# Exponential steps of three and two score tiles in turn, on fixed sets of PSUM banks

## The chip, the cores and the metric

The kernel runs on one core of one Trainium2 chip. Five engines work side by side: TensorE (PE, matmuls; its weight loads are PEld), ScalarE (ACT), VectorE (DVE), GpSimd (POOL) and SyncE (SP, which here only issues DMAs). They share SBUF, and PSUM with eight banks of 512 float32 values on each of 128 partitions. The metric is device time in microseconds of the whole program, the median of several runs.

## What is computed

```python
xn = layernorm(A_x)                                  # 2048 rows x 640
q = (xn @ wq) in 32 heads of 20;  k = xn @ wk;  v = xn @ wv    # one key and value head for all
p = softmax(q k^T * 20**-0.5);  A = concat_heads(p v) @ wo
h = relu(xn @ w1 + b1) ** 2;    B = h @ w2 + b2      # 640 -> 1536 -> 640
out = A_x + A + B
```

The attention is the larger part: 32 heads x 2048 queries x 2048 keys, 134 million exponentials.

## The kernel before

**Tiles.** The work of attention is cut into blocks of four heads and 512 queries: 8 x 4 = 32 blocks. A block has 16 key tiles (kt) of 128 keys. So a block has 64 score tiles (128 keys x 512 queries, exactly one PSUM bank), and the kernel 2048. A score matmul has only 20 rows of contraction, so the array is used in its row mode there, and up to four heads' matmuls run side by side. All other matmuls run in column mode, as four matmuls of 32 columns side by side.

**Two ways to an exponential.** A score tile goes one of two ways:

- ScalarE takes two or three neighbouring banks in one step (`make_act`, line 861) and writes exp as bf16 to the ring `PT` of 20 slots. TensorE then multiplies with the values (`make_pv`), four matmuls for a key tile.
- VectorE approximates: four score tiles of a key tile form a *set*. Each is turned into the bit pattern of a bf16 number by one multiply-add (`D1`, line 1036). Three further patterns are made from all four at once by adding a constant (*passes*, `P1` to `P3`, line 1054, on GpSimd or VectorE). TensorE multiplies all four patterns with scaled values (`make_dpv`), sixteen matmuls for a key tile.

**The value product** of a block collects in one PSUM bank, `PVB` = 7. When all 16 key tiles are in, VectorE copies it out (`TN`, line 929), and small DMAs and VectorE operations divide by the sum of the exponentials. The first value product of the next block waits for that copy.

**Other work** is cut into units: transposes, projections of keys, values and queries, the two layers of the feed-forward part, and the output. A unit takes one PSUM bank, some column matmuls and one eviction by VectorE.

**Order.** Nothing of the order is written out by hand. A planner in the kernel's Python picks one operation after the other with modelled durations and puts it at the end of its engine's queue; the program then has that order for good. The parts that the change touches:

- `make_step` chooses the banks of a step of ScalarE. `STATIC` is off, so it takes any two neighbouring banks of 0 to 6 that come free soonest, or three if at least five are free.
- `pool_banks` gives the banks for VectorE's score tiles (`make_dqk`) and for units: any of 0 to 6.
- When a score step is issued, `make_dqk` may add score tiles for VectorE to it in the same slot of TensorE, until four heads are busy.
- `new_set` opens a set only if enough of the block is left for it to finish. `back` is what GpSimd still has to do; of its queue only passes count.
- `tail_bank` chooses banks for the last half rows of the output.
- Where TensorE would stand idle, the planner adds *fillers*, matmuls of zeros into the open value bank (`fill_parts`), or warm-up matmuls before the first one (`warm_parts`).

All matmuls of these parts are issued through one helper, line 318, so their rows in the profile are told apart by their tiles: `ps<-qT,kT` are scores, `ps<-PT,vx` ScalarE's value products, `ps<-tmore,...` and `ps<-x_sb,...` those of the sets (x_sb's space is reused for patterns), `ps<-kT,zeros` fillers.

Of the kernel before, what the change touches and what calls it, by code (L numbers as in the profile page):

```python
# [16 lines left out]
NBLK = QC * G  # L17
# [18 lines left out]
def _pl(z):  # L36
# [6 lines left out]
XB = (127.0 - EXP_SHIFT * LOG2E - math.log2(TNORM)) * 128.0  # L43

PTR = 20
NB = 7
PVB = 7
SHARED = (4, 5, 6)
STATIC = False
SIDES = ((0, 1), (2, 3))  # L50
POOLED = tuple(range(NB))
HELD = sum(SIDES, ())
EVP = 0.8
JIT = 0.8
# [24 lines left out]
ACTEV = (0, 2)  # L79
KEEP = 1  # L80
DJIT = 9.0
RULES = {}
HOOK = None
PRIO = {'XN1': 0.13}
# [23 lines left out]
MODEL = {}  # L108

DEFAULTS = dict(EVP=EVP, PBIAS=PBIAS, MPRIO=MPRIO, DGAP=DGAP, DLAST=DLAST, DRATE=DRATE, BEHIND=BEHIND, IDLE=IDLE, URG=URG, NOPEN=NOPEN,  # L110
                EPS=0.03, JIT=JIT, R3=R3, STATIC=STATIC, PVA=1, PVD=1, D1P=1, PP=4, SQP=2, DQP=3, QKP=0, ND=2, WARM=WARM, KEEP=KEEP, DJIT=DJIT)


class Ctr:
# [61 lines left out]
def bass_parallel_sum__grouped_kv_mqa__dense_activation_squared_relu__prompt_kernel(nc, A_x, A_wq, A_wk, A_wv, A_wo, B_x, B_w1, B_b1, B_w2, B_b2, out):  # L176
    es = ExitStack()
    with es:
# [276 lines left out]
        DUM = Op("first", "PE", 0.0, [])  # L455

        def fill_parts():
            return [mm(ps[32 * jj:32 * jj + 32, PVB, :], zeros32[:, :], kT[:, 0:512], False, False, (0, 32 * jj)) for jj in range(4)]

        def warm_parts():  # L460
            return [lambda e: e.matmul(ps[:, PVB, :], ones_bf[:, :], hT_tmp[:, 0, :], start=True, stop=True)]

        def need_te(sts):
            return [te_op[st] for st in sts]
# [335 lines left out]
        def make_step():  # L800

            j = len(steps)
            if par("STATIC"):
                banks = list(SIDES[j % 2])
                if any(bank_state(bk) is None for bk in banks):
                    return None
                return build_step(j, banks, 0.0)
            t0 = max(free["PE"], horizon() - par("JIT"))
            st_of = {bk: bank_state(bk) for bk in range(NB)}
            ok = [bk for bk in range(NB) if st_of[bk] is not None and st_of[bk] <= t0 + 0.02]  # L810
            banks = None
            if len(ok) >= 3 + par("R3"):
                ap = [(a, a + d, a + 2 * d) for d in (1,) for a in range(NB - 2 * d) if {a, a + d, a + 2 * d} <= set(ok)]
                if ap:
                    banks = list(ap[0])
            if banks is None:
                can = sorted((max(st_of[bk], st_of[bk + 1], t0), bk) for bk in range(NB - 1) if st_of[bk] is not None and st_of[bk + 1] is not None)
                if not can:
                    return None
                banks = [can[0][1], can[0][1] + 1]  # L820
            return build_step(j, banks, t0)
# [41 lines left out]
        def after_act(st_):  # L863
            for k, t in enumerate(st_["tiles"]):
# [5 lines left out]
                if kt_left[key] == 0:  # L870
                    pv_ready[key[0]].append(("A", key[1]))

        def make_pv(b, kt):
            first, last = b not in pv_begun, pv_count[b] == KT - 1
            parts, deps = [], []
            for h in range(HPG):
                o, sl = tile_act[(b, kt, h)]
                deps.append(o)
                parts.append(mm(ps[32 * h:32 * h + 32, PVB, :], vx[:, kt, :], PT[:, sl, :], first, last, (0, 32 * h)))
            deps.append(v_op[kt // 4])  # L880
            if first and b > 0:
                deps.append(tn_op[b - 1])
            return Op(f"PV{b}_{kt}", "PE", 0.222, parts, deps)

        def make_dpv(s, term):
            b, kt, n = s["b"], s["kt"], s["n"]
            first, last = b not in pv_begun, pv_count[b] == KT - 1 and len(s["terms"]) == 1
            src, wgt = tbuf(s["buf"][term]), (vx if term == 0 else vxs[:, term - 1, :, :])
            deps = list(s["made"][term])
            parts = []  # L890
            for h in range(HPG):
                i = s["order"].index(h)
                parts.append(mm(ps[32 * h:32 * h + 32, PVB, :], wgt[:, kt, :], src[:, i * 512:(i + 1) * 512], first, last, (0, 32 * h)))
            deps.append(v_op[kt // 4])
            if term:
                deps.append(vs_op[kt // 4][term - 1])
            if first and b > 0:
                deps.append(tn_op[b - 1])
            return Op(f"DPV{b}_{kt}_{term}", "PE", 0.2205, parts, deps)

        def finish_pv(b, o):
# [12 lines left out]
        def emit_norm(b, lastpv):  # L914
            marg = DMARG if b < NBLK - 3 else DMEND
            qc, g = divmod(b, G)
            a = b % NOR
            if b >= NBLK - 2:
                Tn, T2 = OR[:, a, :], QCr[:, 0, :]
                tn = op(f"TN{b}", "DVE", 0.63, lambda e: e.transpose(out=Tn, in_=ps[:, PVB, :]), [lastpv] + or_users[a], prio=0)  # L920
                rc = op(f"RC{b}", "DVE", 0.155, lambda e: e.reciprocal(out=Tn[:, DH:512:32], in_=Tn[:, DH:512:32]), [tn], prio=0)
                tm = op(f"TM{b}", "DVE", 0.6, lambda e: e.tensor_tensor(out=T2.rearrange("p (c d) -> p c d", d=32), in0=Tn.rearrange("p (c d) -> p c d", d=32),
                                                                        in1=Tn.rearrange("p (c d) -> p c d", d=32)[:, :, DH:DH + 1].to_broadcast([128, 16, 32]),
                                                                        op=ALU.mult), [rc] + [d for k in qc_dma for d in qc_dma[k]], lock=True, prio=0)
                tn_op[b] = tn
                a = b - NBLK + 2
                tb_op[(qc, NCH - 1 + a)] = op(f"TB{b}", "DVE", 0.63, lambda e: e.transpose(out=OTE[:, a, :], in_=T2), [tm], prio=0)
                return
            tn = op(f"TN{b}", "DVE", 0.60, lambda e: e.tensor_copy(out=OR[:, a, :], in_=ps[:, PVB, :]), [lastpv] + or_users[a], prio=0)
            tn_op[b] = tn  # L930
            d1 = op(f"SM{b}", "SP", 0.58, lambda e: e.dma_start(drs[b, 0].rearrange("(j n) -> j n", j=HPG), OR[DH:128:32, a, :]), [tn], lat=3.1 + marg, dma=nsum[a])
            d2 = op(f"SL{b}", "SP", 0.5, lambda e: e.dma_start(R4[:, a, :], drs[b, 0].rearrange("(p n) -> p n", p=128)), [d1, r4_user.get(a)], lat=1.6 + marg, dma=nr4[a])
# [33 lines left out]
        def new_set():  # L966
            b = cur["b"]
            now = free["PE"]
            opn = sum(1 for s in sets[-NL:] if s["left"])
            back = max(free["POOL"] - now, 0.0) + sum(o.dur for o in pool_q if o.blk is not None) + opn * 1.5 * 1.86  # L970
            need = max(back, HPG * par("DRATE") * (1 + opn)) + par("DLAST")
            if len(unclaimed[b]) * HPG * 0.4523 * 0.85 + DSLACK <= need:
                b += 1
            if b >= NBLK or not (b == 0 or b in qt_op):
                return None
            ok = [kt for kt in unclaimed[b] if kt_ok(kt) and kt // 4 in vs_op]
            if not ok:
# [12 lines left out]
            return s  # L990

        def pool_banks():

            if par("STATIC"):
                return [bk for bk in POOLED if bk not in HELD and bank_state(bk) is not None]
            fb = [bk for bk in POOLED if bank_state(bk) is not None]
            return fb if len(fb) > par("KEEP") else []

        def pick_bank(fb):
# [70 lines left out]
        def tail_bank():  # L1070
            done = not peek_tiles(1)[0]
            bs = [bk for bk in range(NB) if (bk not in HELD or done) and bank_state(bk) is not None]
            if tn_op.get(NBLK - 1) is not None and tn_op[NBLK - 1].fin is not None and not bank_busy[PVB]:
                bank_rel[PVB] = bank_rel[PVB] or tn_op[NBLK - 1]
                bs.append(PVB)
            return min(bs, key=lambda bk: (bank_state(bk), bk)) if bs else None

        def tail_ops():
# [66 lines left out]
        while True:  # L1145
# [34 lines left out]
                if rd is not None and (nq is None or nq > max(free["PE"], rd) + par("DGAP")):  # L1180
                    consider("PE", par("DQP"), r[0], ("dqk",) + r[1:])
            b = pv_blk[0]
            if b < NBLK and (b == 0 or b - 1 in tn_op):
                for k, (kind, x) in enumerate(pv_ready[b]):
                    if kind == "A":
                        consider("PE", par("PVA"), make_pv(b, x), ("pv", b, k))
# [73 lines left out]
            elif kind == "qk":  # L1260
                take_step(ap[1])
                heads = [t[2] for t in ap[1]["tiles"]]
                while len(heads) < HPG:
                    r = make_dqk(heads)
                    if r is None:
# [9 lines left out]
            elif kind == "dqk":  # L1275
                after_dqk(o, *ap[1:])
            elif kind == "pv":
                pv_begun.add(ap[1])
                pv_of[(ap[1], pv_ready[ap[1]].pop(ap[2])[1])] = o
                finish_pv(ap[1], o)  # L1280
            elif kind == "dpv":
                pv_begun.add(ap[1])
                s_, term = ap[3], ap[4]
                s_["pv"][term] = o
                s_["terms"].remove(term)
# [126 lines left out]
```

## Time and profile before

| | before |
|---|---|
| median of 3 runs | 719.19 us (718.53 to 721.15) |
| profiled execution, time and span | 718.53 us, span 716.7 us |
| exponential steps on ScalarE, two tiles and three tiles | 722 and 16 |
| score tiles evicted by VectorE | 556 |
| passes on GpSimd, on VectorE | 216, 201 |
| filler matmuls of zeros | 52 |
| first exponential, start | 14.55 us |
| granted TensorE clock | 1.0 |

How to read the rows: "L861 ACT ACTIVATE PT<-ps 128x1024 x722 | 666.9, 1185 | 7.5" is line, engine, operation, output and input, count, then the time in which the engine was busy with the group, the mean time of one in ns, and the idle time before. Consecutive operations of an engine overlap in part, so the mean of one times the count can exceed the busy time. An "x4" after a matmul counts single matmuls, and four make a group.

### The profile page before, as it was taken

How to read it: one execution, taken by the hardware profiler on the slowest of the kernel's cores; microseconds unless marked ns; L12 is line 12 of the kernel's file. 1: busy time of each engine (PE TensorE's matmuls, PEld its weight loads, DVE VectorE, ACT ScalarE, POOL GpSimd, SP SyncE). 2: the span in 40 equal slices, each digit the busy share in tenths (PEclk: the TensorE clock that was granted, in tenths of full speed). 3: DMA queues.
4: the chain of work that ended last, by engine and by line, in shares of the span. 5: the costliest groups of instructions: out<-in, count | busy, mean ns of one | idle time of the engine just before them, and what ended most of it. 6: DMA issues, size and time to landing. Idle time of an engine off the chain costs nothing.

```text
span 716.7 us, 22623 instructions
## 1 busy us (share of the span) xinstructions
PE 705.8 (98%) x9787; PEld 219.6 (31%) x9789; DVE 642.5 (90%) x1100; ACT 694.1 (97%) x760; POOL 439.3 (61%) x274
## 2 busy tenths in 40 slices
PE   8999999999999999999999999999999999999998
PEld 4422222233322223333322223333333222233234
DVE  7879999998999989897999989999999999999973
ACT  6899999999999999999999999999999899999994
POOL 3727667758577664564457457667757557575643
PEclk9999999999999999999999999999999999999999
DMA  6416411332357501112110001101111100221101
GB/s 197 116 51 172 117 35 58 99 92 57 97 107 159 140 17 26 41 54 57 39 27 19 24 22 28 49 22 47 29 49 47 29 21 22 90 56 28 53 17 48
DMA packets 42016, 44.01 MB, mean 61 GB/s; under 512 B 15540, under 2 KB 32772, under 8 KB 41788
## 3 DMA queue, kind: packets, MB, share of 16 engines
q1 hardware_dynamic: 39132, 36.93, 18.9%
q0 software_dynamic: 2208, 5.25, 3.5%
q8 instruction: 77, 1.26, 0.7%
q10 hardware_dynamic: 576, 0.38, 0.2%
q14 instruction: 23, 0.19, 0.1%
HBM read 28.03 MB, written 14.91 MB: 60 GB/s over the span
## 4 chain that ended last, share of the span: by engine, by line
ACT 71%; PE 25%; DVE 2%; DMA 1%; issue 0%; SPq 0%
ACT PT L861 71%; PE ps L318 24%; DVE tmore L1036 1%; DMA x_sb<-in_A_x_dram 1%; PE ps L491 1%; DVE tmore L1054 0%; PE ps L519 0%; DVE x_sb L1054 0%; PE ps L447 0%; ACT OC L372 0%; SPq L335 0%; DVE OC L955 0%; PE ps L426 0%; SPq L342 0%; ACT xnT L428 0%
## 5 line engine op out<-in xcount | busy, mean ns | idle before, releaser
L861 ACT ACTIVATE PT<-ps 128x1024 bf16<-128x1024 f32 (+1 forms) x738 | 684.3, 1194 | 8.5 <-PE ps L318 8.3
L1036 DVE TENSOR_SCALAR tmore<-ps 128x512 uint16<-128x512 f32 x556 | 358.8, 682 | 36.6 <-PE ps L318 33.1
L1054 POOL TENSOR_SCALAR tmore<-tmore 128x2048 uint16<-128x2048 uint16 x115 | 217.1, 1896 | 154.3 <-PE ps L318 57.3
L318 PE MATMUL ps<-qT,kT 20*128 20x512 bf16 x2048 | 291.3, 384 | 4.4 <-ACT PT L861 3.0
L1054 POOL TENSOR_SCALAR x_sb<-tmore 128x2048 uint16<-128x2048 uint16 x101 | 190.6, 1896 | 88.7 <-DVE x_sb L1054 34.2
L318 PEld LDWEIGHTS ps<-qT,kT 20*128 20x128 bf16 x2048 | 74.3, 91 | 289.7 <-ACT PT L861 239.3
L318 PE MATMUL ps<-PT,vx 128*32 128x512 bf16 x1492 | 138.2, 386 | 0.0
L1054 DVE TENSOR_SCALAR x_sb<-tmore 128x2048 uint16<-128x2048 uint16 x129 | 98.8, 794 | 0.5 <-PE ps L318 0.5
L318 PE MATMUL ps<-x_sb,vxs 128*32 128x512 bf16 x920 | 82.5, 382 | 0.0
L318 PE MATMUL ps<-w_sb,big 128*32 128x320 bf16 x1536 | 77.3, 302 | 0.3 <-DVE tmore L1036 0.3
L318 PE MATMUL ps<-xnT,w_sb 128*32 128x512 bf16 x960 | 75.9, 384 | 0.5 <-ACT PT L861 0.4
L318 PE MATMUL ps<-tmore,vxs 128*32 128x512 bf16 x748 | 67.4, 382 | 0.0
L318 PEld LDWEIGHTS ps<-PT,vx 128*32 128x32 bf16 x1492 | 35.9, 94 | 61.5 <-issue 54.4
L318 PE MATMUL ps<-tmore,vx 128*32 128x512 bf16 x556 | 54.4, 383 | 0.0
L1054 DVE TENSOR_SCALAR tmore<-tmore 128x2048 uint16<-128x2048 uint16 x72 | 53.1, 750 | 0.2 <-PE ps L318 0.2
L318 PEld LDWEIGHTS ps<-w_sb,big 128*32 128x32 bf16 x1536 | 31.6, 95 | 32.0 <-issue 24.7
L599 DVE TENSOR_SCALAR hT_tmp<-ps,b1col 128x512 bf16<-128x512 f32 x48 | 35.7, 745 | 3.7 <-PE ps L318 3.4
L318 PE MATMUL ps<-xnT,wq_sb 128*32 128x512 bf16 (+1 forms) x480 | 34.1, 356 | 0.0
L318 PE MATMUL ps<-wo_c,OC 128*32 128x320 bf16 x608 | 31.1, 301 | 0.0
L607 DVE TENSOR_TENSOR big<-hT_tmp 128x512 bf16<-128x512 bf16 x48 | 27.0, 573 | 0.2
L318 PEld LDWEIGHTS ps<-x_sb,vxs 128*32 128x32 bf16 x920 | 21.4, 95 | 18.8 <-issue 12.9
L318 PEld LDWEIGHTS ps<-xnT,w_sb 128*32 128x32 bf16 x960 | 17.8, 94 | 28.0 <-issue 22.5
(82 smaller groups left out, 263.3 us busy)
## 6 DMA issues: line engine op xcount, KB each, us to landing
xbd<-b2d SPq DMA_DIRECT2D x16, 320.0 KB, 4.3
xbd<-in_A_x_dram POOLq DMA_DIRECT2D x8, 640.0 KB, 6.7
xr<-xbd SPq DMA_DIRECT2D x32, 160.0 KB, 2.4
w_sb<-in_B_w_dram SPq DMA_DIRECT2D x8, 480.0 KB, 4.7
big<-OR SPq DMA_DIRECT2D x71, 40.0 KB
big<-drs SPq DMA_DIRECT2D x71, 40.0 KB
out_dram<-out_sb SPq DMA_DIRECT2D x15, 160.0 KB, 1.9
qT<-QCr SPq DMA_DIRECT2D x108, 20.0 KB
```

Source lines behind the costliest of these rows:

```text
L318: return lambda e: e.matmul(out_, l, r, start=start, stop=stop, tile_position=tp)
L491: return [(lambda e, dt=dt: e.transpose(out=psbf(bk)[:, dt * 128:(dt + 1) * 128], in_=xn_sb[:, st, dt:D:DT], identity=ident[:])) for dt in ...
L599: o = Op(f"RL{qc}_{f}", "DVE", 0.66, [lambda e: e.tensor_scalar(out=hT_tmp[:, k % 2, :], in0=ps[:, bk, :], scalar1=b1col[:, f:f + 1], scal ...
L607: q = op(f"SQ{qc}_{f}", "DVE", 0.34, lambda e: e.tensor_tensor(out=h2T[:, f, :], in0=hT_tmp[:, k % 2, :], in1=hT_tmp[:, k % 2, :], op=ALU. ...
L861: return Op(f"ACT{st_['j']}", "ACT", 0.05 + 0.4267 * n, [lambda e: e.activation(out=PT[:, s0:s0 + n, :], in_=ps[:, b0:b0 + (n - 1) * db + ...
L1036: d1 = op(f"D1_{n}_{i}", "DVE", 0.60, lambda e: e.tensor_scalar(out=L[:, cs].bitcast(U16), in0=ps[:, bank, :], scalar1=XA, scalar2=XB, op0 ...
L1054: p = op(f"P{j}_{n}", eng, 0.60 if eng == "DVE" else 1.86, lambda e, T=T, j=j, two=two: e.tensor_scalar(out=T.bitcast(U16), in0=L.bitcast( ...
```

## The change

The eight banks are split for good. Banks 0, 1, 2 and banks 3, 4 are two sets (`SIDES`) that ScalarE's steps take in turn, three tiles and two tiles; banks 5, 6, 7 are for VectorE's score tiles, for units and for the value product. The value product has no fixed bank any more: at the first product of a block `bank_for` chooses one of the three, `kept` keeps it from other use before that, and the first product waits for that bank's last reader. `back` counts everything that GpSimd has queued. The tail may use any of the eight banks. `DV` belongs to a branch that joins two steps of two and that runs only with `STATIC` off.

```diff
-NB = 7
-PVB = 7
+NB = 8
+PV0 = 7
 SHARED = (4, 5, 6)
-STATIC = False
-SIDES = ((0, 1), (2, 3))
+STATIC = True
+SIDES = ((0, 1, 2), (3, 4))
 POOLED = tuple(range(NB))
 HELD = sum(SIDES, ())
...
+DV = 9
+D1P = 1
...
+        pv_bank = {0: PV0}
+        bank_busy[PV0] = True
+
+        def bank_for(b):
+
+            if b in pv_bank:
+                return pv_bank[b]
+            can = [(bank_state(bk), -bk) for bk in range(NB) if bank_state(bk) is not None and not (par("STATIC") and bk in HELD)]
+            return -min(can)[1] if can else None
+
+        def kept():
+
+            b = pv_blk[0]
+            return bank_for(b) if b < NBLK and b not in pv_begun else None
+
+        def pv_begin(b):
+            if b not in pv_begun:
+                pv_bank[b] = bank_for(b)
+                bank_busy[pv_bank[b]] = True
+                pv_begun.add(b)
...
-            if first and b > 0:
-                deps.append(tn_op[b - 1])
+            if first:
+                deps.append(bank_rel[bank])
...
+            tn.frees = pb
...
-            back = max(free["POOL"] - now, 0.0) + sum(o.dur for o in pool_q if o.blk is not None) + opn * 1.5 * 1.86
+            back = max(free["POOL"] - now, 0.0) + sum(o.dur for o in pool_q) + opn * 1.5 * 1.86
...
+            keep = kept()
             if par("STATIC"):
-                return [bk for bk in POOLED if bk not in HELD and bank_state(bk) is not None]
-            fb = [bk for bk in POOLED if bank_state(bk) is not None]
+                return [bk for bk in POOLED if bk not in HELD and bk != keep and bank_state(bk) is not None]
+            fb = [bk for bk in POOLED if bk != keep and bank_state(bk) is not None]
...
             bs = [bk for bk in range(NB) if (bk not in HELD or done) and bank_state(bk) is not None]
-            if tn_op.get(NBLK - 1) is not None and tn_op[NBLK - 1].fin is not None and not bank_busy[PVB]:
-                bank_rel[PVB] = bank_rel[PVB] or tn_op[NBLK - 1]
-                bs.append(PVB)
...
-            if b < NBLK and (b == 0 or b - 1 in tn_op):
+            if b < NBLK and (b == 0 or b - 1 in tn_op) and bank_for(b) is not None:
```

With `STATIC` on, `make_step` takes the banks from `SIDES`, and a step is possible only when the whole set of its turn is free in the planner's books:

```python
            if par("STATIC"):
                banks = list(SIDES[j % 2])
                if any(bank_state(bk) is None for bk in banks):
                    return None
                return build_step(j, banks, 0.0)
```

More of the change, by code (lines that the diff above doesn't have):

```diff
@@ L110 @@
 DEFAULTS = dict(EVP=EVP, PBIAS=PBIAS, MPRIO=MPRIO, DGAP=DGAP, DLAST=DLAST, DRATE=DRATE, BEHIND=BEHIND, IDLE=IDLE, URG=URG, NOPEN=NOPEN,
-                EPS=0.03, JIT=JIT, R3=R3, STATIC=STATIC, PVA=1, PVD=1, D1P=1, PP=4, SQP=2, DQP=3, QKP=0, ND=2, WARM=WARM, KEEP=KEEP, DJIT=DJIT)
+                EPS=0.03, JIT=JIT, R3=R3, STATIC=STATIC, PVA=1, PVD=1, D1P=D1P, PP=4, SQP=2, DQP=3, QKP=0, ND=2, WARM=WARM, KEEP=KEEP, DJIT=DJIT, DV=DV)
 class Ctr:
@@ L457, in fill_parts @@
         def fill_parts():
-            return [mm(ps[32 * jj:32 * jj + 32, PVB, :], zeros32[:, :], kT[:, 0:512], False, False, (0, 32 * jj)) for jj in range(4)]
+            return [mm(ps[32 * jj:32 * jj + 32, pv_bank[pv_blk[0]], :], zeros32[:, :], kT[:, 0:512], False, False, (0, 32 * jj)) for jj in range(4)]
         def warm_parts():
-            return [lambda e: e.matmul(ps[:, PVB, :], ones_bf[:, :], hT_tmp[:, 0, :], start=True, stop=True)]
+            return [lambda e: e.matmul(ps[:, PV0, :], ones_bf[:, :], hT_tmp[:, 0, :], start=True, stop=True)]
         def need_te(sts):
@@ L808, in make_step @@
             t0 = max(free["PE"], horizon() - par("JIT"))
-            st_of = {bk: bank_state(bk) for bk in range(NB)}
+            keep = kept()
+            st_of = {bk: bank_state(bk) if bk != keep else None for bk in range(NB)}
             ok = [bk for bk in range(NB) if st_of[bk] is not None and st_of[bk] <= t0 + 0.02]
@@ L875, in make_pv @@
             parts, deps = [], []
+            bank = bank_for(b)
             for h in range(HPG):
@@ L878, in make_pv @@
                 deps.append(o)
-                parts.append(mm(ps[32 * h:32 * h + 32, PVB, :], vx[:, kt, :], PT[:, sl, :], first, last, (0, 32 * h)))
+                parts.append(mm(ps[32 * h:32 * h + 32, bank, :], vx[:, kt, :], PT[:, sl, :], first, last, (0, 32 * h)))
             deps.append(v_op[kt // 4])
-            if first and b > 0:
-                deps.append(tn_op[b - 1])
+            if first:
+                deps.append(bank_rel[bank])
             return Op(f"PV{b}_{kt}", "PE", 0.222, parts, deps)
@@ L890, in make_dpv @@
             parts = []
+            bank = bank_for(b)
             for h in range(HPG):
                 i = s["order"].index(h)
-                parts.append(mm(ps[32 * h:32 * h + 32, PVB, :], wgt[:, kt, :], src[:, i * 512:(i + 1) * 512], first, last, (0, 32 * h)))
+                parts.append(mm(ps[32 * h:32 * h + 32, bank, :], wgt[:, kt, :], src[:, i * 512:(i + 1) * 512], first, last, (0, 32 * h)))
             deps.append(v_op[kt // 4])
@@ L896, in make_dpv @@
                 deps.append(vs_op[kt // 4][term - 1])
-            if first and b > 0:
-                deps.append(tn_op[b - 1])
+            if first:
+                deps.append(bank_rel[bank])
             return Op(f"DPV{b}_{kt}_{term}", "PE", 0.2205, parts, deps)
@@ L917, in emit_norm @@
             a = b % NOR
+            pb = pv_bank[b]
             if b >= NBLK - 2:
                 Tn, T2 = OR[:, a, :], QCr[:, 0, :]
-                tn = op(f"TN{b}", "DVE", 0.63, lambda e: e.transpose(out=Tn, in_=ps[:, PVB, :]), [lastpv] + or_users[a], prio=0)
+                tn = op(f"TN{b}", "DVE", 0.63, lambda e: e.transpose(out=Tn, in_=ps[:, pb, :]), [lastpv] + or_users[a], prio=0)
+                tn.frees = pb
                 rc = op(f"RC{b}", "DVE", 0.155, lambda e: e.reciprocal(out=Tn[:, DH:512:32], in_=Tn[:, DH:512:32]), [tn], prio=0)
@@ L928, in emit_norm @@
                 return
-            tn = op(f"TN{b}", "DVE", 0.60, lambda e: e.tensor_copy(out=OR[:, a, :], in_=ps[:, PVB, :]), [lastpv] + or_users[a], prio=0)
+            tn = op(f"TN{b}", "DVE", 0.60, lambda e: e.tensor_copy(out=OR[:, a, :], in_=ps[:, pb, :]), [lastpv] + or_users[a], prio=0)
+            tn.frees = pb
             tn_op[b] = tn
@@ L992, in pool_banks @@
         def pool_banks():
+            keep = kept()
             if par("STATIC"):
-                return [bk for bk in POOLED if bk not in HELD and bank_state(bk) is not None]
-            fb = [bk for bk in POOLED if bank_state(bk) is not None]
+                return [bk for bk in POOLED if bk not in HELD and bk != keep and bank_state(bk) is not None]
+            fb = [bk for bk in POOLED if bk != keep and bank_state(bk) is not None]
             return fb if len(fb) > par("KEEP") else []
@@ L1262, in bass_parallel_sum__grouped_kv_mqa__dense_activation_squared_relu__prompt_kernel @@
                 heads = [t[2] for t in ap[1]["tiles"]]
+                if len(heads) == 2 and not par("STATIC") and sum(1 for bk in POOLED if bank_state(bk) is not None and bank_state(bk) <= o.start + 0.06) >= par("DV"):
+                    can = [bk for bk in range(NB - 1) if all(k != kept() and bank_state(k) is not None and bank_state(k) <= o.start + 0.06 for k in (bk, bk + 1))]
+                    st_ = build_step(len(steps), [can[0], can[0] + 1], 0.0) if can else None
+                    if st_ is not None and len(st_["tiles"]) == 2 and not set(t[2] for t in st_["tiles"]) & set(heads):
+                        rd = st_["qk"].ready()
+                        if rd is not None and rd <= o.start + 0.06:
+                            st_["qk"].dur = 0.005
+                            commit(st_["qk"])
+                            st_["qk"].lat = 0.425
+                            take_step(st_)
+                            heads += [t[2] for t in st_["tiles"]]
                 while len(heads) < HPG:
@@ L1277, in bass_parallel_sum__grouped_kv_mqa__dense_activation_squared_relu__prompt_kernel @@
             elif kind == "pv":
-                pv_begun.add(ap[1])
+                pv_begin(ap[1])
                 pv_of[(ap[1], pv_ready[ap[1]].pop(ap[2])[1])] = o
@@ L1281, in bass_parallel_sum__grouped_kv_mqa__dense_activation_squared_relu__prompt_kernel @@
             elif kind == "dpv":
-                pv_begun.add(ap[1])
+                pv_begin(ap[1])
                 s_, term = ap[3], ap[4]
```

## The prediction

> **What bounds the kernel now.** I read the page's busy times first.
>
> ```profile
> PE 705.8 (98%) x9787; PEld 219.6 (31%) x9789; DVE 642.5 (90%) x1100; ACT 694.1 (97%) x760; POOL 439.3 (61%) x274
> ```
>
> ScalarE (ACT) and TensorE (PE) are both full, so I need to know which of them a step of the loop waits for. The groups with shapes kept apart give ScalarE's two kinds of step (two and three tiles of 512 scores) and VectorE's eviction of a score tile:
>
> ```profile
> L861 ACT ACTIVATE PT<-ps 128x1024 bf16<-128x1024 f32 x722 | 666.9, 1185 | 7.5 <-PE ps L318 7.3
> L861 ACT ACTIVATE PT<-ps 128x1536 bf16<-128x1536 f32 x16 | 25.5, 1593 | 1.0 <-PE ps L318 1.0
> L1036 DVE TENSOR_SCALAR tmore<-ps 128x512 uint16<-128x512 f32 x556 | 358.8, 682 | 36.6 <-PE ps L318 33.1
> ```
>
> 722 x 2 + 16 x 3 = 1492 tiles go through ScalarE and 556 through VectorE, together 2048. The mean of a step is longer than its share of the busy time, because the write of one step overlaps the read of the next. What counts is the distance from start to start, and the chain that ended last gives it:
>
> ```profile
> 39.97 243.76 ACT PT L861 x263
> ...
> 354.95 165.05 ACT PT L861 x179
> ...
> 520.04 31.68 PE ps L318 x451
> ...
> 709.07 4.15 PE ps L318 x116
> ```
>
> By the trace's records six of the 263 steps and two of the 179 have three tiles. So 257a + 6b = 243.76 and 177a + 2b = 165.05, which gives a = 0.918 us for a step of two and b = 1.33 us for a step of three. The single records agree: a step of three is followed after 1.330 us in most of the sixteen cases, a step of two at best after 0.904 us. A tile more costs 0.426 us, an instruction more only 0.904 - 2 x 0.426 = 0.052 us. The stretch from 520 us shows that TensorE ends the chain in places. The waits say who is late:
>
> ```profile
> PEld ps L318 <- ACT PT L861: 242.8, 610, 0.8
> ...
> PEld ps L318 <- DVE tmore L1036: 15.1, 45, 0.6
> ...
> ACT PT L861 <- PE ps L318: 8.3, 7, 2.1
> ```
>
> Score matmuls wait for ScalarE 610 times, mostly to be allowed into a bank that ScalarE is still reading. ScalarE stood idle for TensorE only 7 times. Last, the timeline of TensorE around one score step:
>
> ```profile
> 159.03 0.39 PE L318 MATMUL ps<-tmore,vxs 128*32 128x512 bf16 x4
> ...
> 159.35 0.39 PE L318 MATMUL ps<-qT,kT 20*128 20x512 bf16 x2
> ...
> 159.67 0.40 PE L318 MATMUL ps<-PT,vx 128*32 128x512 bf16 x4
> ...
> 159.89 0.39 PE L318 MATMUL ps<-tmore,vx 128*32 128x512 bf16 x4
> ```
>
> A group of four column matmuls takes 0.22 us (159.67 to 159.89). From the group before the score step to the one after are 0.64 us, so a score step costs 0.42 us, with its two changes of the array's mode. Before, 942 groups of 512 columns for the value products and fillers and 340 for projections, 1282 x 0.2225 = 285 us, and 552 groups of 320 columns x 0.138 = 76 us, make 0.490 us a step; with 0.42 that is 0.91 us, which is ScalarE's own pace. The two are balanced.
>
> **The change part by part.** The order of the built program settles the counts. ScalarE has 320 steps of three and 320 of two, 1600 tiles: 108 more than before, in 98 fewer instructions. VectorE has 448 evictions at line 1036 for 556 (112 sets for 139), and GpSimd 137 passes for 216, VectorE's own passes 199 for 201.
>
> *More tiles on ScalarE.* Why: three of eight banks are left to all else, one of them holds the running value product, and the rule that opens a set now counts all that GpSimd has queued. Cost on the path: 108 x 0.426 = 46.0 us, less 98 x 0.052 = 5.1 us, is 40.9 us. ScalarE is busy without a break for most of the span, so nothing hides it.
> The page "ScalarE: Activation LUTs" of the Trainium skill, section Rules for kernel authors, budgets about 0.3 us per ACTIVATE plus 0.83 ns per element. By its fixed part 98 fewer instructions would give back 29 us and leave the kernel only some 16 us slower, an estimate from that page. Back to back, this trace shows 0.052 us, since most of the fixed part lies under the next step, and I go by the trace.
>
> *Less on VectorE and GpSimd.* 108 evictions x 0.682 = 74 us and 79 passes x 1.896 (mean of GpSimd's passes) = 150 us go away. Both engines already wait for others, so this is worth nothing directly; what is late next is still ScalarE.
>
> *TensorE.* 98 score steps x 0.42 = 41 us fall away, and 27 sets x 4 value groups become 27 x 1, so 81 x 0.2225 = 18 us. The planner fills the room: filler groups against zeros rise from 13 to 234, 221 x 0.2225 = 49 us. In a pair of steps TensorE has 1082 + 340 groups x 0.2225 and 552 x 0.138, over 320 pairs 1.227 us, and 2 x 0.42, together 2.07 us against ScalarE's 0.904 + 1.330 = 2.234. TensorE falls from 100% to 93% of ScalarE's pace: it no longer sets the pace, and its gain is worth only the two places (331 and 562 us) where the trace shows ScalarE waiting 2 to 3 us for it.
>
> *Fixed bank sets.* A bank must be refilled while ScalarE works on the other set. By the records, a score matmul starts at the earliest 0.055 us after the step that frees its bank has ended, takes 0.388 us, and the next step starts 0.041 us later, together 0.484 us. Before, a step ends 1.19 us after its start and its bank is due at 2 x 0.904 = 1.808 us, so 0.13 us are to spare. After, the set of three ends at 1.61 us and is due at 2.234: 0.14 us to spare. The set of two has 0.56 us. So the tight turn is no tighter, and there is one in two steps. ScalarE's loss to this kind of lateness is in a = 0.918 already (0.014 us a step), and I keep it; bounds for it are 0 and the in-flight group of rival two. Behind a waiting score step TensorE holds value products and fillers; ScalarE needs those value products only to reuse its 20 output slots, four pairs later, 8.9 us.
>
> *Value bank chosen per block.* The first value product of a block no longer waits for the copy of the block before (L929, 0.685 us), but for its new bank. At most 31 x 0.69 = 21 us of TensorE's time, at least nothing; hidden under ScalarE either way, so nothing. If ScalarE's cover were gone it would be a gain.
>
> *Start and end.* The first exponential stands at 14.55 us and what precedes it is unchanged. In its first 40 steps the kernel before loses 3.7 us against ScalarE's bare pace, waiting for keys; after has the same transposes and key projections, and I keep 3.7 (2 to 8). After the last exponential the kernel before needs 11.31 us. In the chain 116 matmuls (29 groups, 4.15 us) follow the last transpose of the output; after, 14 groups do, since seven of eight half rows wait ready. Then VectorE's six evictions of 0.49 us set the end, about 1.0 us earlier: 10.3 us. The DMA counts of SP's and GpSimd's queues are the same throughout.
>
> *No effect.* The new DV branch runs only with fixed sets off, and D1P keeps its value: nothing.
>
> **The sum.** 14.55 + 320 x (0.918 + 1.330) = 719.4, less 0.92 because the last step counts with its own 1.2 us in place of the distance to a next, + 3.7 at the start, + 5 for places where TensorE or VectorE is late (before: about 8 us in such places; after has more room on both engines; 0 to 15), + 10.3 at the end: 753.2 us of span. The profiled run before took 718.53 us for a span of 716.7, so 1.83 more: 755.1. Its median is 719.19, 1.0009 times that: **755.7 us**, 5% slower.
>
> **The rivals.** *One, not slower:* a step of three is cheaper than its row, say because a whole set on neighbouring banks runs better in rotation. With no idle time at all, 716.7 - 14.55 - 10.3 - 1.2 + 0.92 = 691.6 us are left for 320 pairs, 2.161 us each, so the third tile would have to cost 0.353 us or less. Below that the change wins. The sixteen steps of three and the two chain stretches both say 0.426; 2%.
>
> *Two, slower still:* the refill of three banks comes late. If a column group (0.22 us) is in flight whenever the set comes free, the score step starts up to 0.2 us later than the 0.14 to spare allows, plus 0.10 for the change of mode: 0.08 to 0.18 us a pair, 27 to 58 us, so 781 to 812 us. Against it: the same spare time before cost 0.014 us a step with TensorE full. 6%.
>
> *Three, slower by less:* score tiles for VectorE share a slot with ScalarE's and wait for two banks only. TensorE waited 15.1 us for VectorE's evictions with seven banks in common; up to twice that, on the path, gives 765 to 785 us. VectorE is less loaded, which speaks against it. 9%.
>
> *Four:* TensorE's clock. The granted clock is 9 or more in all slices, with TensorE 98% busy; warm-up matmuls in the first microseconds follow each other by 0.427 us, later by 0.216. If a twentieth of the span ran like that, 16 pairs would need up to 2 x 2.07 = 4.1 us for 2.23, some 30 us more: about 786 us. The fillers speak against it. 3%.
> "TensorE: Matmul & The Clock Gate" in the Trainium skill, section A second HAM failure mode, warns that short idle times between matmul groups while cycling through PSUM banks can bring the clock down again. No slice of this trace shows it.
>
> **How the numbers follow.** My forecast has 80%, from 746 (bare pace of 2.234 a pair, 2.5 at the start, nothing lost later: 742.5 + 1.83 + 0.7 = 745) to 765. To leave no more than 2 in 10 out, the range goes up into rival three: 746 to 770. A measurement here can tell about 0.5%, 3.6 us, from no change. Slower by more: 0.98; within: 0.01; faster: 0.01, since only rival one reaches there.
>
> **What would show it.** In the profile after: 320 + 320 ACT rows at L861's successor with 1.19 and 1.6 us means; ScalarE's busy time near 735 us of a span near 753; a chain that is ScalarE for over 85%, in pieces of 1.12 us per step (2.248 a pair); TensorE with its idle share up although fillers stand in it; VectorE near 76% busy (642.5 - 108 x 0.645 = 573 us). I am wrong if the chain's pieces show under 1.08 us a step (rival one), if ScalarE's idle time behind score matmuls passes 25 us (two or three, told apart by whether these matmuls wait for ACT or for DVE), or if the clock shows a slice below 9.

## The result and the profile after

The changed kernel takes 753.14 us (median of 3 runs, 753.05 to 753.17) against 719.19: a ratio of 1.0465, 95% interval 1.0434 to 1.0497. The profiled run has a span of 751.4 us and took 753.17 us. The forecast was 755.7 us. The ratios, here and below, are to runs of the kernel before taken at the same time and leave out one slow run each of the fourth and the eleventh experiment, so they are not quite the quotient of the two medians.

The page's busy times and granted clock, after:

```profile
PE 716.6 (95%) x10359; PEld 241.2 (32%) x10361; DVE 580.0 (77%) x990; ACT 733.5 (98%) x662; POOL 292.0 (39%) x195
...
PEclk9999999999999999999999999999999999999999
```

ScalarE is busy 39 us longer with 98 fewer instructions, VectorE and GpSimd shed 63 and 147 us, and TensorE's clock stays full. The groups with shapes kept apart show the two kinds of step in equal number, and VectorE's evictions, which now wait 112 us for score tiles (36.6 before):

```profile
L864 ACT ACTIVATE PT<-ps 128x1536 bf16<-128x1536 f32 x320 | 522.6, 1633 | 4.9 <-PE ps L320 4.9
L864 ACT ACTIVATE PT<-ps 128x1024 bf16<-128x1024 f32 x320 | 388.6, 1214 | 1.4 <-PE ps L320 1.4
L1066 DVE TENSOR_SCALAR tmore<-ps 128x512 uint16<-128x512 f32 x448 | 299.5, 686 | 112.3 <-PE ps L320 109.7
```

The chain that ended last has become one piece from 41 us on; before, TensorE cut it in several places:

```profile
41.23 698.48 ACT PT L864 x618
```

618 steps are 309 pairs, so a pair takes 2.260 us. The waits say that hardly anything of this is idle time of ScalarE; the four waits in its row all lie before 41.3 us:

```profile
PEld ps L320 <- ACT PT L864: 272.2, 630, 1.2
...
ACT PT L864 <- PE ps L320: 6.3, 4, 2.7
PEld ps L320 <- DVE tmore L1066: 5.0, 20, 0.4
```

TensorE waits for ScalarE more than before (272 us for 243) and for VectorE less (5.0 us for 15.1).

### The profile page after: what moved, and what is told of

Same layout as the page of the kernel before. It is cut to its first block, busy times and chain, and to the rows that moved or that the text cites. A ratio compares the mean times of both kernels' runs of the same rounds, so it can differ in the third digit from the quotient of the medians.

```text
span 751.4 us, 23326 instructions
## 1 busy us (share of the span) xinstructions
PE 716.6 (95%) x10359; PEld 241.2 (32%) x10361; DVE 580.0 (77%) x990; ACT 733.5 (98%) x662; POOL 292.0 (39%) x195
## 3 DMA queue, kind: packets, MB, share of 16 engines
q8 instruction: 81, 1.33, 0.7%
## 4 chain that ended last, share of the span: by engine, by line
ACT 94%; PE 4%; DMA 1%; DVE 1%; SPq 0%; issue 0%; DVEq 0%
ACT PT L864 94%; PE ps L320 3%; DMA x_sb<-in_A_x_dram 1%; PE ps L463 0%; PE ps L493 0%; DVE out_sb L1144 0%; PE ps L521 0%; PE ps L449 0%; ACT OC L374 0%; SPq L337 0%; DVE OR L379 0%; DVE kT L507 0%; PE ps L428 0%; SPq L344 0%; ACT xnT L430 0%
## 5 line engine op out<-in xcount | busy, mean ns | idle before, releaser
L864 ACT ACTIVATE PT<-ps 128x1536 bf16<-128x1536 f32 (+1 forms) x640 | 723.8, 1424 | 6.4 <-PE ps L320 6.3
L1066 DVE TENSOR_SCALAR tmore<-ps 128x512 uint16<-128x512 f32 x448 | 299.5, 686 | 112.3 <-PE ps L320 109.7
L320 PE MATMUL ps<-qT,kT 20*128 20x512 bf16 x2048 | 267.9, 384 | 27.7 <-ACT PT L864 24.8
L1084 POOL TENSOR_SCALAR tmore<-tmore 128x2048 uint16<-128x2048 uint16 x81 | 153.4, 1898 | 242.4 <-DVE x_sb L1084 85.8
L1084 POOL TENSOR_SCALAR x_sb<-tmore 128x2048 uint16<-128x2048 uint16 x56 | 106.4, 1902 | 169.6 <-DVE x_sb L1084 114.5
L320 PE MATMUL ps<-PT,vx 128*32 128x512 bf16 x1600 | 152.9, 387 | 0.6 <-DVE OR L957 0.5
L320 PE MATMUL ps<-kT,zeros 128*32 128x512 bf16 x936 | 74.9, 381 | 0.0
L320 PE MATMUL ps<-x_sb,vxs 128*32 128x512 bf16 x740 | 65.9, 382 | 0.2
L320 PE MATMUL ps<-tmore,vxs 128*32 128x512 bf16 x604 | 52.3, 381 | 0.0
L320 PEld LDWEIGHTS ps<-kT,zeros 128*32 128x32 bf16 x936 | 21.7, 95 | 21.7 <-issue 12.6
L320 PEld LDWEIGHTS ps<-xnT,w_sb 128*32 128x32 bf16 x960 | 20.5, 95 | 25.2 <-issue 13.6
```

Source lines behind the costliest of these rows:

```text
L320: return lambda e: e.matmul(out_, l, r, start=start, stop=stop, tile_position=tp)
L864: return Op(f"ACT{st_['j']}", "ACT", 0.05 + 0.4267 * n, [lambda e: e.activation(out=PT[:, s0:s0 + n, :], in_=ps[:, b0:b0 + (n - 1) * db + ...
L1066: d1 = op(f"D1_{n}_{i}", "DVE", 0.60, lambda e: e.tensor_scalar(out=L[:, cs].bitcast(U16), in0=ps[:, bank, :], scalar1=XA, scalar2=XB, op0 ...
L1084: p = op(f"P{j}_{n}", eng, 0.60 if eng == "DVE" else 1.86, lambda e, T=T, j=j, two=two: e.tensor_scalar(out=T.bitcast(U16), in0=L.bitcast( ...
```

## The experiments

The measure that runs through all of them is the *bare pace*: the number of two-tile steps x 0.904 us plus three-tile steps x 1.330 us. The theory: the tiles that are left to ScalarE set the time, and the set layout matters only through their number. Rivals: the fixed sets cost by themselves; the moved value bank matters; the clock.

One part of the change needs no run. With the old `back` (only passes counted) the built program is the same in every queue, so this edit does nothing here.

**Fixed sets, but two and two.** Four banks are left to the rest.

```diff
-SIDES = ((0, 1, 2), (3, 4))
+SIDES = ((0, 1), (2, 3))
```

> The changed kernel with SIDES = ((0, 1), (2, 3)): fixed sets of two and two banks, four banks for the rest, value bank still chosen per block. The built program has 748 steps of two tiles (1496 tiles) and 552 evictions by VectorE; ScalarE's bare pace is 748 x 0.904 = 676.2 us, and the two kernels measured so far lie 38 us (after) to 45 us (before) above theirs. Theory (the tiles that ScalarE has to take set the time): 714 to 721 us. Rival (fixed sets themselves cost, because a step cannot move to a bank that is free; spare time in a turn is 0.13 us): each of 748 turns loses 0.03 us or more, 740 us and up.

Measured: 721.6 us, ratio to before 1.0033 (1.0021 to 1.0045), 45.4 us above its bare pace where before is 45.2 above its own. Its ScalarE waits, by the waits view, are

```profile
ACT PT L864 <- PE ps L320: 6.1, 4, 2.8
```

So fixed sets are not what costs: 748 turns with 0.13 us to spare lose together no more than before. The time is 0.6 us above the range that was expected, and 2.2 us of the excess over before is the four additional tiles (bare pace 676.2 for 674.0).

**The value bank alone.**

```diff
-STATIC = True
+STATIC = False
```

> The changed kernel with STATIC = False: of the change only the value bank chosen per block (and eight banks in one pool) is left. 719 steps of two and 18 of three, 1492 tiles as before, 556 evictions; bare pace 673.9 us. Theory (a value bank of its own choice is worth nothing, since ScalarE covers it): 716 to 721 us, within 0.4% of before. Rival (the removed wait for the copy was worth up to 21 us of TensorE's time in a kernel where TensorE is as full as ScalarE): 700 to 712 us.

Measured: 723.87 us, 1.0056 (1.0040 to 1.0072): 0.6% slower, which neither reading expected. The stretch by stretch view (busy times of PE, PEld, DVE, ACT and POOL; the last three columns are granted clock, DMA share and GB/s) finds one cause:

```profile
250.00:256.00 6.00, 5.12 (x61) 1.36 (x53) 5.74 (x11) 6.00 (x8) 3.77 (x3) 1.00 0.07 14
256.00:264.00 8.00, 8.00 (x67) 1.61 (x69) 6.77 (x11) 5.60 (x7) 3.65 (x2) 0.57 0.01 2
```

For 6.8 us TensorE runs at half clock. 67 matmuls take 8 us, and ScalarE is busy for 5.60 of 8. This is a part of the loss only: four of the six runs had a mean clock of 0.995 and took 723.8 to 724.3 us, the other two had 0.999 and 1.0 and took 721.4 and 721.9. Two further places, near 312 and 336 us, lose about 3 us each with the clock at 1.00 and TensorE busy throughout: dense groups of other work, as the kernel before has at 331 and 562 us.

**No more than 112 sets, banks as before.** This takes the number of tiles of the changed kernel into the old layout, by two lines in `new_set`.

```diff
             ok = [kt for kt in unclaimed[b] if kt_ok(kt) and kt // 4 in vs_op]
+            if len(sets) >= 112 / NBLK * (cur['b'] + 1.0 - len(unclaimed[cur['b']]) / KT) + 1:
+                return None
             if not ok:
                 return None
```

> The kernel before, all banks shared as they were, but no more sets opened than 112/32 per block: 448 evictions and 1600 tiles on ScalarE, as in the changed kernel, in 738 steps of two, 41 of three and one of one. Bare pace 722.2 us. Theory (tiles on ScalarE alone set the time): 722.2 + 38 to 45 = 760 to 767 us, slower than the changed kernel by its 140 more instructions x 0.052 = 7 us. Rival (the layout of the banks costs, the lower number of sets is only a by-product with room to spare): 719 to 730 us.

Measured: 770.28 us, 1.0711 (1.0694 to 1.0728). The rival is out: with banks to spare, 1600 tiles cost 51 us. The time is 3 us above the range. The mean clock was 0.987, which is 2 x 0.013 x 767.5 = 20 us at half speed (the traces of this case show the clock at full or at half, nothing between).

**No fillers.**

```diff
-WARM = 0.72
+WARM = 0.0
```

> The changed kernel with WARM = 0: no filler groups of zeros after the start (884 fewer matmuls than in the kernel as changed counted from before, none of them left). The planner then finds 115 sets, 318 steps of three, 317 of two; bare pace 709.5 us. Theory (fillers fill idle time of TensorE and cost nothing, and TensorE is busy enough without them): 709.5 + 38 = 748 us with the granted clock at 9 in all slices. Rival a (fillers hold the clock): slices below 9 and over 760 us. Rival b (fillers delay score steps): the gap above the bare pace shrinks from 38 us to 33 us or less, below 743 us.

Measured: 794.43 us (784.3 to 798.75), 1.0999 (1.0945 to 1.1053), with a bare pace 5 us *lower* than the changed kernel's. Rival a held. The page's clock row, and the waits of ScalarE:

```profile
PEclk9999779979999797999989699999897669997669
```

```profile
ACT PT L864 <- PE ps L320: 42.8, 50, 2.7
```

The mean clock is 0.894, so 2 x 0.106 x 791.6 = 168 us ran at half speed, and ScalarE waited 42.8 us for TensorE in place of 6.3. One passage, stretch by stretch:

```profile
80.00:88.00 8.00, 7.55 (x101) 2.15 (x97) 5.24 (x9) 8.00 (x8) 0.46 (x1) 1.00 0.37 98
88.00:96.00 8.00, 7.33 (x54) 1.52 (x51) 4.69 (x9) 6.65 (x6) 6.03 (x4) 0.55 0.18 60
96.00:104.00 8.00, 8.00 (x64) 1.60 (x60) 4.10 (x7) 4.95 (x4) 1.02 (x1) 0.50 0.01 2
```

Matmuls fall from 101 to 54 in 8 us, and ScalarE from 8.00 us busy to 4.95 two rows on. TensorE still looks busy (7.33 and 8.00): its busy share does not tell a full clock from a half one.

**Fixed sets with the old value bank.** The kernel before with two lines changed.

```diff
-STATIC = False
-SIDES = ((0, 1), (2, 3))
+STATIC = True
+SIDES = ((0, 1, 2), (3, 4))
```

> The kernel before with the fixed sets alone: STATIC = True and SIDES = ((0, 1, 2), (3, 4)), the value product still in bank 7, so banks 5 and 6 for all else. 318 steps of three, 317 of two, 1588 tiles, 460 evictions, 736 filler matmuls; bare pace 709.5 us. Theory (two free banks give about as few sets whichever bank holds the values, and the tiles set the time): 709.5 + 38 = 748 us, 744 to 752. Rival (the value bank chosen per block is what made the changed kernel's end and turns cheap): 755 us and more.

Measured: 755.76 us, 1.0520 (1.0499 to 1.0540), with the clock at 0.991 (14 us at half speed). So the fixed sets of three and two account for the whole loss without the value bank. It lies in the rival's range, 7.8 us above the theory's 748, but its half-clock passages explain most of that: by the trace, ScalarE loses 6.6 us to its bare pace between 100 and 200 us, where the longest of them lies (1.4 us in that stretch of the changed kernel), and 1.0 to 1.5 us in each 100 us from there to 700 us. Whether the moved bank is worth anything is not settled by it.

**A few more sets in the changed kernel.**

```diff
-DGAP = 0.5
+DGAP = 0.1
-WARM = 0.72
+WARM = 0.8
```

> The changed kernel with DGAP = 0.1 (VectorE's score tiles are issued more readily between steps) and WARM = 0.8: 117 sets in place of 112, 316 steps of three and of two, 1580 tiles, 468 evictions, 792 filler matmuls; bare pace 705.9 us, 9.0 us under the changed kernel's 714.9. Theory: 744 us, 741 to 747, the whole 9 us, since VectorE and GpSimd have room. Rival (more score tiles of VectorE on two banks make TensorE wait for evictions): 750 us and more.

Measured: 748.39 us, 1.0423 (1.0405 to 1.0441): 4.8 us less than the changed kernel for 9.0 expected. The direction follows the tiles; the clock (0.988, 18 us at half speed) took much of the rest back: by the trace, ScalarE loses 6.1 us to its bare pace between 500 and 600 us, where the page's clock row dips, and 1.2 us in that stretch of the changed kernel.

**Value bank alone, more fillers.** `WARM = 0.85` in the second experiment.

> The second experiment (shared banks, value bank chosen per block) with WARM = 0.85: fillers are added at a higher threshold, 164 matmuls of zeros for 116; 715 steps of two and 18 of three, 564 evictions, bare pace 670.3 us. The second experiment lost time in one stretch at half clock (6.8 us) and in bursts where ScalarE waits. Theory (the half clock and what follows it was its loss): no slice below 9 and 716 us, 713 to 719, level with or below before. Rival (the moving value bank costs in itself): again 50 us above the bare pace, 720 us and more, with the clock at 9 throughout.

Measured: 719.21 us, 1.0008 (0.9998 to 1.0017), clock at 9 in all slices. It is 4.7 us below the second experiment, but 3.6 us of that are ScalarE's fewer tiles, and the gap to the bare pace is still 48.9 us, as the rival said. The time itself lies between the two ranges (up to 719, and from 720 on). The chain of this run is 74% TensorE. So with shared banks the value bank gains nothing; the kernel stays limited by TensorE.

**The cap with more fillers.** `WARM = 0.85` in the third experiment.

> The third experiment (no more than 112 sets, shared banks) with WARM = 0.85: 728 matmuls of zeros for 524, 732 steps of two and 45 of three, again 1600 tiles, bare pace 722.1 us. Theory (20 us at half clock were the reason for 770 us in place of 760 to 767): no slice below 9 and 762 us, 759 to 766. Rival (the rest of the gap is lateness that comes with shared banks): 768 us and more with the clock at 9.

Measured: 761.97 us, 1.0608 (1.0594 to 1.0623), clock at 9 in all slices: the theory's number. With 1600 tiles and a full clock, shared banks lie 39.9 us above the bare pace, the fixed sets of the changed kernel 38.2. The 8.8 us between the two kernels are the 7.2 us of bare pace (138 more instructions) and 1.7 of all else.

**More fillers in the changed kernel.** `WARM = 0.85`.

> The changed kernel with WARM = 0.85: the same 320 steps of three and 320 of two, the same 448 evictions, but 1244 matmuls of zeros for 936, 77 groups x 0.2225 = 17 us more on TensorE. Theory (with one set of banks waiting there is room on TensorE; fillers cost nothing at this level): 753 us, 751 to 755. Rival (fillers in front of score steps delay them): up to 17 us more, 758 to 770 us.

Measured: 753.48 us, 1.0476 (1.0456 to 1.0496). 17 us more of matmuls on TensorE cost 0.3 us.

**A shorter lookahead in the kernel before.**

```diff
-JIT = 0.8
+JIT = 0.6
-WARM = 0.72
+WARM = 0.85
```

> The kernel before with JIT = 0.6 (a step's banks are chosen later, so that VectorE's score tiles find banks) and WARM = 0.85: 675 steps of two, 43 of three, one of one; 1480 tiles, 568 evictions, 372 matmuls of zeros; bare pace 667.9 us, 6 us under before. Theory (tiles set the time, if TensorE keeps up): 667.9 + 45 = 713 us. Rival (TensorE is at its limit and the shorter lookahead leaves ScalarE waiting): 718 us and more, with ScalarE's idle time up and the gap to the bare pace at 50 us or more.

Measured: 733.36 us, 1.0196 (1.0173 to 1.0219), though it has 12 tiles fewer on ScalarE. The gap to the bare pace rises to 65 us, and ScalarE's waits for TensorE to

```profile
ACT PT L861 <- PE ps L318: 17.4, 22, 2.8
```

The rival held: fewer tiles help only while score steps come in time. Here the chain is 81% TensorE. Two things qualify this. The lookahead and the fillers were changed together, and 80 more filler groups x 0.2225 = 18 us fall on an engine that was full; the run does not tell the two apart. And part of the loss is one accident: a transfer stands in the chain,

```profile
193.35 12.79 DMA R<-drs
```

TensorE then waits 2.1 us, and 10 us at half clock follow (the mean is 0.993). ScalarE loses 9.0 us to its bare pace between 200 and 300 us, but also 3.1 to 5.8 us in each other 100 us from 100 to 700, where the kernel before loses 1.3 to 3.5. The next experiment shows what such a transfer is.

**Fixed sets of two and two, more sets.** The first experiment with `DLAST = 6.0`.

> The first experiment (fixed sets of two and two) with DLAST = 6.0, so that sets may be opened closer to a block's end: 744 steps of two, 1488 tiles, 560 evictions, 56 matmuls of zeros; bare pace 672.6 us, 3.6 us under the first experiment's. Theory: 721.6 - 3.6 = 718.0 us, 716.5 to 719.5, level with before. Rival (with fewer fillers the clock falls, or VectorE's later sets hold up the blocks' ends): 722 us and more.

Measured: 731.21 us, 1.0158 (1.0136 to 1.0180), 13 us off. The chain, in order of time, names a transfer that no theory had:

```profile
214.90 15.29 DMA R<-drs
```

It reads the row sums of a block back (8 KB; the median of 30 such reads is 1.9 us in this run). The stretches tell what stood beside it and what followed:

```profile
220.00:226.00 6.00, 6.00 (x79) 1.58 (x71) 4.42 (x8) 6.00 (x8) 3.48 (x3) 1.00 0.98 164
226.00:233.00 7.00, 3.06 (x26) 0.56 (x23) 2.58 (x5) 2.36 (x3) 2.73 (x3) 0.83 0.71 158
233.00:250.00 17.00, 17.00 (x135) 3.15 (x131) 10.12 (x17) 11.82 (x12) 8.58 (x5) 0.57 0.26 57
```

The DMA engines were 98% busy: GpSimd issued 640 KB transfers (x added onto the bias rows) at 206.5, 212.7, 214.9 and 223.9 us. The reciprocal behind the small read waited 5.0 us in VectorE's queue, the eviction behind it kept TensorE waiting for 4.2 us, and ScalarE for 4.9. Then the clock was halved, and 17 us passed with ScalarE busy for 11.8. By the trace ScalarE lost 12.2 us to its bare pace between 200 and 300 us, and 1.3 in the same stretch of the first experiment. The next experiment takes the collision away.

**The same with the transfers spread.** Only their start is moved.

```diff
-            xb=[f"RL0_{k}" for k in range(6)] + ["RL3_3", "RL3_5"])
+            xb=[f"RL0_{2 * k}" for k in range(6)] + ["RL3_3", "RL3_5"])
```

> The eleventh experiment with the 640 KB transfers of GpSimd spread: six of them are held until the feed-forward units 0, 2, 4, 6, 8, 10 in place of 0 to 5, so that they start about twice as far apart. 746 steps of two, 1492 tiles, 556 evictions; bare pace 674.4 us. Theory (the read of the row sums waited 15 us behind these transfers, and the clock fell because of that wait): no read of row sums over 6 us, no slice of the clock below 9, and 674.4 + 45.4 = 720 us, 718 to 722. Rival (DLAST = 6.0 itself makes VectorE late at the ends of blocks): again 728 us or more, with VectorE waiting several us in one place.

Measured: 717.81 us, 0.9997 (0.9988 to 1.0006), clock at 9 in all slices, no wait of VectorE for a read of row sums. One read still took 8.9 us, over the 6 us of the theory, but nothing waited for it; in the first experiment one took 9.9 us, and VectorE waited 0.2 us. So the eleventh experiment's loss was the collision and the clock after it. This kernel has fixed sets, a value bank chosen per block, exactly the tiles of the kernel before (1492), and its time. It is level; no version here beats the kernel before.

## Why the prediction was right

*More tiles on ScalarE: 40.9 us.* This is the cause. ScalarE's busy time rose by 39.4 us. The third experiment reaches the same number of tiles with shared banks and is slower still; the twelfth keeps fixed sets with 1492 tiles and is level with before; the fifth needs nothing but the two fixed sets. Of the two reasons that the prediction gave for the fewer sets, the scarce banks hold (138 sets in the first experiment, with four banks for the rest, 112 with three); the rule with GpSimd's queue is wrong, as the unchanged program shows.

*The price of an instruction, 0.052 us.* The page's 0.3 us per ACTIVATE, which its row gives for a bias held as a `[128,1]` pointer operand where this kernel has a plain number, would have made the loss some 16 us; it was 34. The eighth experiment has 138 instructions more than the changed kernel for the same tiles and the same full clock, and lies 8.8 us above it. By 0.3 us each that would be 41 us.

*The pace.* A pair was put at 2.248 us plus 5 us in all for late places, which is 2.264; the chain shows 2.260. The trace's records give 7.8 us over the bare pace after 41 us, for 4.5 (0.014 us for each of 320 pairs) + 5 in the sum. That 5 was set against 8 us of the kernel before, which its trace does not bear out: of the 8.3 us in its waits row 4.7 lie before 41 us. After 41 us it loses 12.8 us in all, and 0.014 us for each of 698 steps of two is 9.8 of them, so some 3 us are left.

*The start: 14.55 and 3.7 us; it was 14.72 and 5.1.* This term was too small. ScalarE's timeline shows its waits in brackets at the end of a line, first before,

```profile
14.55 7.44 ACT L861 ACTIVATE PT<-ps 128x1024 bf16<-128x1024 f32 x8 [1.97 <-PE ps L318]
22.57 2.11 ACT L861 ACTIVATE PT<-ps 128x1024 bf16<-128x1024 f32 x2 [0.57 <-PE ps L318]
```

then after, with two long waits of 2.69 and 1.43 us:

```profile
14.72 6.88 ACT L864 ACTIVATE PT<-ps 128x1536 bf16<-128x1536 f32 x6 [1.98 <-PE ps L320]
24.30 6.88 ACT L864 ACTIVATE PT<-ps 128x1536 bf16<-128x1536 f32 x6 [2.69 <-PE ps L320]
...
41.23 1.02 ACT L864 ACTIVATE PT<-ps 128x1024 bf16<-128x1024 f32 x1 [1.43 <-PE ps L320]
```

Six steps eat 15 of the first 16 tiles, the seventh needs three and so a new key tile, and stops a whole step; before, the eighth step was the last that needed no new keys.

*The end: 10.3 us; it was 8.5.* Also mis-sized. The last exponential ends at 742.9 us. The timeline of VectorE after it, below the same transpose before, where the last exponential ended at 705.4 us:

```profile
706.53 0.72 DVE L920 STREAM_TRANSPOSE OR<-ps 128x512 f32<-128x512 f32 x1 [0.16 <-PE ps L318]
```

```profile
743.38 0.72 DVE L947 STREAM_TRANSPOSE OR<-ps 128x512 f32<-128x512 f32 x1 [12.06 <-PE ps L320]
...
746.43 1.69 DVE L1144 TENSOR_TENSOR out_sb<-ps,w_sb 128x320 bf16<-128x320 f32 x4 [0.56 <-PE ps L320]
```

The first transpose follows 0.5 us after the last exponential, 1.15 us before: the last group to be added is now a value product of ScalarE's own tiles, where in the kernel before the product of one of GpSimd's passes came last. And evictions follow each other by 0.42 us (four in 1.69), not by their duration of 0.49. The start came out 1.6 us over its term and the end 1.8 under it, so that together they are 0.2 us under the forecast; that they cancel is luck. The late places are 1.7 us under.

*TensorE and VectorE: nothing.* Right to within a few us. By the trace's records ScalarE loses 12.8 us to its bare pace between 41 us and its last exponential in the kernel before and 7.8 us after, so the room on TensorE can have returned 5.0 of the 40.9 us at most. The two places at 331 and 562 us, where ScalarE waits 1.39 and 2.15 us by the records (not 2 to 3), are in that. How much of it comes from the smaller number of sets is not shown: at full clock the same loss is 9.0 and 8.9 us in the first and the twelfth experiment (138 and 139 sets), but 18.6 us in the seventh (141), and 9.9 and 7.9 us in the eighth and the ninth (112). The gaps to the bare pace differ more than that because they hold the end as well: after the last exponential come 11.3 us before, 15.0 and 12.8 us in the first and the twelfth, and 8.5 us in the kernels of 112 sets at full clock.

*The value bank: nothing.* With shared banks it was 0.6% slower once and level once, never faster. Its own worth stays open, since each edit makes the planner build another order.

*The rivals.* The one that would have won needed a third tile for 0.353 us or less; 320 steps of three keep the pace at 1.33. Late refills of three banks needed 0.08 to 0.18 us a pair on top of 2.248; the pair took 2.260. Waits for VectorE's evictions are out by the waits after (5.0 us). Number four, the clock, has the right mechanism: without the fillers the kernel loses some 40 us more. The section A second HAM failure mode in the skill's "TensorE: Matmul & The Clock Gate" tells of a kernel whose clock kept changing between half and full because TensorE was idle only briefly, but often, between groups of matmuls. The fourth experiment agrees as far as it goes: 168 us ran at half clock, although no pause of TensorE after the start was longer than 0.95 us. The length of a pause alone does not decide it, since the changed kernel has pauses of 0.87 us at full clock. There the 234 filler groups prevented it, as the prediction's 3% supposed.

## What to carry to other kernels

When two engines share one kind of work, price a layout by where it sends the work: a wider step saved 0.05 us an instruction, and the banks it took cost 0.43 us for every tile that the other engine no longer got. Find the pace of back-to-back instructions from the distance between their starts, multiply by the counts of the built program, and put it beside the measured time; the gap then tells what else is going on. Idle time on TensorE is not free room until the granted clock has been read beside it.

## What had not been expected of the hardware

Seven of the twelve experiments had a mean clock of 0.995 or less in the profiled run: 7 us (second) to 168 us (fourth) at half speed, with TensorE's busy share at 94% to 99% on the page. Most of the passages at half clock begin after a few us in which TensorE worked with gaps, and one wait of 4.2 us in the eleventh experiment was followed by 17 us at half speed. But the longest passage of the sixth, from 581.1 us on, began after TensorE had been busy for 7.05 of 7.1 us, though with only 71 matmuls in that time (118 in the 8 us before). What exactly takes the clock down stays open. Once down it stays so for 3.4 us or a multiple: inside these seven runs the passages last 3.4, 6.8, 10.2, 13.7, 17.1 or 20.5 us. Nor is it the program alone: of eleven runs of the kernel before that were taken beside the ninth to eleventh experiment, eight had a mean clock of 0.999 or 1.0 and took 718.5 to 719.2 us, the others 0.995, 0.991 and 0.988 and took 722.2, 725.0 and 727.6.

A read of 8 KB with a median of 1.9 us took 15.3 us beside 640 KB transfers. The same read took 12.8 us in the tenth experiment and 8.8 us in the fifth, and there too a wait of TensorE (2.1 and 1.6 us) and 10 us at half clock followed. Fillers worth 17 us of TensorE's time cost 0.3 us, the absence of all fillers some 40 us.
